# Windowed decode attention with a gated branch: keys turned by VectorE, scores from added shares, two kv heads a unit

## The chip, the cores and the metric

The kernel runs on one core of a Trainium2 chip. The metric is device time in microseconds (us) of one execution. TensorE is PE in the profile (PEld its weight loads), VectorE is DVE, ScalarE is ACT, GpSimd is POOL, and SyncE is SP, which issues nearly all loads here. Everything is float32. PSUM has eight banks of 512 floats a partition.

## The reference

Two tokens (batch 2, one query each) are normalised; one branch attends over the last 4096 keys of a long cache, the other makes a gate.

```
xn = layernorm(x)                                 # x: 2 x 1 x 512
q = xn @ wq                                       # 32 heads of 128
k, v = caches[:, :, -4096:, :]                    # 8 kv heads, 4 query heads each
o = softmax(q @ k.T / sqrt(128)) @ v              # per head
s = o @ wo                                        # 4096 -> 512
z = gelu(xn @ w_in)                               # 1792 wide, halves z1, z2
g = silu((z1 * (w_sp * layernorm(z2) + b_sp)) @ w_out)
out = x + s * g
```

The keys and values used are 2 x 8 x 4096 x 128 floats each, 67.1 MB together; w_in, w_out, wq and wo are 22.3 MB.

## The kernel before, in words

Everything on PE, DVE, ACT and SP is kept in program order by a small wrapper (lines 26 to 38), so the order in the source is the order on each engine. All large loads go through SP's queue into one ring of nine slots of 16 KB a partition (line 74): two halves of w_in, w_out, four quarters of wq, then for each of 16 pairs (batch, kv head) its keys and its values (`load_kv`, line 118), 2 MB each, 16 KB a partition, then wo in seven pieces. A load goes out when the slot's last user is done.

At the start x is normalised and turned; z is made in four pieces of 448 columns, whose four shares are added while PE turns them (28 small products, lines 206 to 210). The products of `queries(0)` to `queries(3)`, one for each quarter of wq, are put between the steps of the gate's branch. Then q is turned on PE into qT.

The loop over pairs (lines 420 to 443) works on pair `cur` while it finishes pair `prev`. For `cur`: 32 transposes of 128x128 on PE (`transposes`, eight groups of four, each into one of three "kt" banks), each group copied to SBUF by DVE or ACT (ON_ACT, line 306); then `scores` (eight products, four column groups of PE beside each other), `row_max` on DVE over 1024 scores, `share_max` on PE. For `prev`: `bias`, `probs` (one exponential of 128x1024 on ACT), `probs_t` (two block transposes of 128x512 on DVE), `share_sum` and `weights`, `pv` (eight products), `evacuate` (four scaled copies on ACT), and one pair later `collect`. So the softmax of one pair and the transposes of the next lie beside each other.

wo is used in three sets of rows (line 296), each with its own turned output (`spread`), so that most of its products can be done before the last pair is through. 24 of the 32 blocks are added in one bank (`part`), the others follow into `so`; then the gate, the addition of x, and two stores.

Of the kernel before, what the change touches and what calls it, by code (L numbers as in the profile page):

```python
# [14 lines left out]
P = 128  # L15
HQ, DH = 32, 128
G = 4
EPS = 1e-5


def free_ap(t, offset, dims):

    return bass.AP(tensor=t.tensor, offset=t.offset + offset, ap=[list(t.ap[0])] + [list(d) for d in dims])
# [18 lines left out]
def kernel(  # L42
# [19 lines left out]
    NT = W // P  # L62
    NR = W // 512 // G
# [3 lines left out]
    FC = F // G  # L67
    FT = FH // P
    NJ = HQ * DH // P
    DC = D // G  # L70
    SCALE = DH ** -0.5

    cst = ctx.enter_context(tc.tile_pool(name="cst", bufs=1))
    ring = ctx.enter_context(tc.tile_pool(name="ring", bufs=9))
# [3 lines left out]
    def slot(name, *shape):  # L78
        return ring.tile([P, *shape], F32, tag="slot", name=name)

    def bank(name, *shape):
        return ps.tile([P, *shape], F32, tag="kt", name=name, bufs=3)


    xs = sb.tile([B, D], F32, tag="o", name="xs")
    act.dma_start(xs, x[:, 0, :])
    win_v = w_in.rearrange("(p k) f -> p k f", p=P)
    win = []
    for a in range(2):
        t = slot(f"win{a}", 2, F)  # L90
        sp.dma_start(t, win_v[:, 2 * a : 2 * a + 2, :])
        win.append(t)
    wout = slot("wout", FT, D)
    sp.dma_start(wout, w_out.rearrange("(p j) d -> p j d", p=P))
    wq_v = wq.rearrange("(p k) f -> p k f", p=P)
    wqt = []
    for a in range(KT):
        t = slot(f"wq{a}", HQ * DH)
        sp.dma_start(t, wq_v[:, a, :])
        wqt.append(t)  # L100
# [4 lines left out]
    x4 = cst.tile([P, DC], F32, tag="x4", name="x4")  # L105
    nc.gpsimd.memset(x4, 0.0)
# [4 lines left out]
    def load_x4():  # L111
        h = DC // 2
        src = bass.AP(tensor=x.tensor, offset=x.offset, ap=[[DC, G], [D, B], [1, h]])
        sp.dma_start(x4[0 : P : P // (G * B), :h], src)
        for b in range(B):
            sp.dma_start(x4[16 * b : P : 32, h:], by_group(x, b, h, DC))

    def load_kv(n):
        b, kv = divmod(n, HKV)
        pair = []  # L120
        for name, src in (("k", k_cache), ("v", v_cache)):
            t = slot(f"{name}{n}", NT, DH)
            sp.dma_start(t, src[b, kv, SK - W :, :].rearrange("(p j) d -> p j d", p=P))
            pair.append(t)
        return pair


    ident = cst.tile([P, P], F32, tag="ident", name="ident")
    make_identity(nc, ident)
    selw = cst.tile([P, 60], F32, tag="selw", name="selw")  # L130
    nc.gpsimd.memset(selw, 0.0)
    xnT = cst.tile([P, KT, 32], F32, tag="xnT", name="xnT")
    nc.gpsimd.memset(xnT, 0.0)
    ones = cst.tile([P, P], F32, tag="ones", name="ones")
    nc.gpsimd.memset(ones, 1.0)
    hT = cst.tile([P, FT, 32], F32, tag="hT", name="hT")
    nc.gpsimd.memset(hT, 0.0)
    qT = cst.tile([P, B * HKV, 32], F32, tag="qT", name="qT")
    nc.gpsimd.memset(qT, 0.0)

    rowm = cst.tile([P, 32], F32, tag="rowm", name="rowm")
    dve.tensor_reduce(rowm, ident.rearrange("p (g c) -> p c g", g=G), axis=AX.X, op=ALU.add)
    grpm = cst.tile([P, G], F32, tag="grpm", name="grpm")
# [20 lines left out]
    xn = sb.tile([B, D], F32, tag="o", name="xn")  # L164
    dve.tensor_scalar(xn, xs, mv[:, 0:1], rs, op0=ALU.subtract, op1=ALU.mult)
    pt = bank("xnT_ps", KT, B)
# [3 lines left out]

    same = cst.tile([P, G, 32], F32, tag="same", name="same")
    dve.tensor_copy(same, free_ap(rowm, 0, [[0, G], [1, 32]]))
    heads = cst.tile([P, 32, REP], F32, tag="heads", name="heads")
    dve.tensor_copy(heads, free_ap(rowm, 0, [[0, 32], [8, REP]]))
    diag = cst.tile([P, 4], F32, tag="diag", name="diag")
    dve.tensor_reduce(diag, free_ap(rowm, 0, [[4, 4], [1, REP]]), axis=AX.X, op=ALU.add)
    dve.tensor_reduce(selw[:, 28:32], free_ap(rowm, 0, [[1, REP], [4, 4]]), axis=AX.X, op=ALU.add)
    perm8 = cst.tile([P, 4, 8, 4, 4], F32, tag="perm8", name="perm8")
    nc.gpsimd.memset(perm8, 0.0)
    for i in range(4):  # L180
        dve.tensor_copy(perm8[:, i, :, :, i], free_ap(ident, 0, [[1, 8], [32, 4]]))
    perm16 = cst.tile([P, 2, 16, 4, 2], F32, tag="perm16", name="perm16")
    nc.gpsimd.memset(perm16, 0.0)
    for i in range(2):
        dve.tensor_copy(perm16[:, i, :, :, i], free_ap(ident, 0, [[1, 16], [32, 4]]))

    assert KT == G
    z = sb.tile([P, F], F32, tag="kts", name="z")  # L190
    for n in range(G):
        pz = bank(f"z{n}", 512)[:, :FC]
        for k in range(KT):
            pe.matmul(
                pz[32 * k : 32 * k + 32, :], xnT[:, k, :], win[k // 2][:, k % 2, n * FC : (n + 1) * FC],
                start=True, stop=True,
            )
        if n % 2:
            dve.tensor_copy(z[:, n * FC : (n + 1) * FC], pz)
        else:  # L200
            act.activation(z[:, n * FC : (n + 1) * FC], pz, AF.Copy)
    wb_ps = ps.tile([P, 512], F32, tag="mo", name="wb_ps")[:, :2]
    pe.matmul(wb_ps, ones[0:1, :], wb1, start=True, stop=True)
    wb = cst.tile([P, 2], F32, tag="wb", name="wb")
    dve.tensor_copy(wb, wb_ps)
    pt = bank("zT_ps", 2, FT, B)
    zv = z.rearrange("b (h p j) -> b h j p", h=2, j=FT)
    for h in range(2):
        for j in range(FT):
            pe.matmul(pt[:, h, j, :], zv[:, h, j, :], rowm[:, :B], start=True, stop=True)  # L210


    assert HKV == NR * G
    pq = ps.tile([P, NR, 512], F32, tag="s", name="q_ps")

    def queries(k):
        for r in range(NR):
            for g in range(G):
                c = (r * G + g) * 512
                pe.matmul(  # L220
                    pq[32 * g : 32 * g + 32, r, :], xnT[:, k, :], wqt[k][:, c : c + 512],
                    start=(k == 0), stop=(k == KT - 1),
                )

    queries(0)
    zT = cst.tile([P, 2, FT, B], F32, tag="zT", name="zT")
    dve.tensor_copy(zT, pt)
    u = cst.tile([P, 2, FT, B], F32, tag="u", name="u")
    dve.tensor_mul(u, zT, zT)
    dve.tensor_scalar(u, u, 0.044715, 1.0, op0=ALU.mult, op1=ALU.add)  # L230
    dve.tensor_mul(u, u, zT)
    dve.tensor_scalar(u, u, -2.0 * math.sqrt(2.0 / math.pi), 80.0, op0=ALU.mult, op1=ALU.min)
    act.activation(u, u, AF.Exp)
    dve.tensor_scalar_add(u, u, 1.0)
    dve.reciprocal(u, u)
    dve.tensor_mul(zT, zT, u)

    z1, z2, w2 = zT[:, 0], zT[:, 1], u[:, 0]
    mean = cst.tile([P, B], F32, tag="mean", name="mean")
    var = cst.tile([P, B], F32, tag="var", name="var")  # L240

    def mean_over_rows(dst, src, name):
        pm = bank(name, FT, B)
        pe.matmul(pm.rearrange("p j b -> p (j b)"), ones, src.rearrange("p j b -> p (j b)"), start=True, stop=True)
        dve.reduce_sum(dst, pm.rearrange("p j b -> p b j"), axis=AX.X)
# [3 lines left out]
    queries(1)  # L249
    dve.tensor_scalar_mul(mean, mean, 1.0 / FH)  # L250
    dve.tensor_sub(z2, z2, free_ap(mean, 0, per_b))
# [4 lines left out]
    dve.tensor_mul(z2, z2, free_ap(mean, 0, per_b))  # L256
    dve.tensor_scalar(z2, z2, wb[:, 0:1], wb[:, 1:2], op0=ALU.mult, op1=ALU.add)
    dve.tensor_mul(hT[:, :, 0 : 16 * B : 16], z1, z2)
    queries(2)
    y = bank("y", DC)  # L260
    for j in range(FT):
        for g in range(G):
            pe.matmul(
                y[32 * g : 32 * g + 32, :], hT[:, j, :], wout[:, j, g * DC : (g + 1) * DC],
                start=(j == 0), stop=(j == FT - 1),
            )
    gate = cst.tile([P, DC], F32, tag="gate", name="gate")
# [6 lines left out]
    queries(3)  # L274
    qs = sb.tile([P, NR, REP, DH], F32, tag="kts", name="qs")
    for r in range(NR):
        dve.tensor_copy(qs[:, r], pq[:, r, :].rearrange("p (i d) -> p i d", i=REP))
    for r in range(NR):
        pt = bank(f"qT_ps{r}", REP, G, 32)
        for i in range(REP):  # L280
            pe.transpose(pt[:, i].rearrange("p g c -> p (g c)"), qs[:, r, i, :], ident)
        for b in range(B):
            dve.tensor_copy(
                qT[:, b * HKV + r * G : b * HKV + r * G + G, ::8], pt[:, :, :, b].rearrange("p i g -> p g i")
            )

    NP = B * HKV
    JH = NT // NR
    acc = ps.tile([P, 4, DH], F32, tag="acc", name="acc")
    dve.memset(acc, 0.0)

    SETS = ((0, 4, 16), (4, 2, 8), (6, 2, 8))
    sets = {}
    for i, (kv, n, nj) in enumerate(SETS):
        o1 = cst.tile([P, B, 32], F32, tag=f"o1_{i}", name=f"o1_{i}")
        oT = cst.tile([P, nj, 32], F32, tag=f"oT_{i}", name=f"oT_{i}")  # L300
        nc.gpsimd.memset(oT, 0.0)
        for a in range(n):
            sets[kv + a] = (a, n, o1)
# [231 lines left out]
```

## Time and profile before

| | |
|---|---|
| Runs | 219.18, 220.66 (median), 221.65 us |
| Span of the profiled execution, first to last instruction | 217.7 us |
| Time of that execution itself | not kept beside its span |
| Instructions | 3816 |
| Busy: PE, DVE, ACT | 176.7, 109.4, 80.5 us |
| Read from HBM | 89.40 MB |
| Loads in flight, issue to landing (values, median) | 36.3 us |

In the profile's rows the engine comes first, then what is written from what is read, its shape, and either a count with the busy time and the mean of one in ns, or a start and a length in us. Brackets at the end of a timeline row are the time that the engine stood idle before it, and who ended that. In a table by stretches the figures are the stretch, its length, busy time (with count) of PE, PEld, DVE, ACT and POOL, the granted TensorE clock as a share of full speed, the share of DMA and GB/s. A float32 product is two records of PE.

### The profile page before, as it was taken

To read this page: it belongs to the slowest core of one execution; us is meant where nothing else is said; L and a number is where in the kernel's file an instruction comes from. 1 tells how busy PE (TensorE), PEld (TensorE's weight loads), DVE (VectorE), ACT (ScalarE), POOL (GpSimd) and SP (SyncE) were. 2 spreads that over 40 slices of the span, in tenths; PEclk is the share of its full clock that TensorE was granted. 3 is DMA by queue.
4 is the path that set the end of the run, shared out by engine and by line. 5 is a ranking of instruction groups with operands and counts; after the bars stand their busy time and mean duration, and the time that the engine had idled before them with its cause. 6 is when DMAs were issued, how large, how long until landed. Compare 5 with 4: busy or idle time off the path is not lost.

```text
span 217.7 us, 3816 instructions
## 1 busy us (share of the span) xinstructions
PE 176.7 (81%) x1554; PEld 105.2 (48%) x1554; DVE 109.4 (50%) x259; ACT 80.5 (37%) x173; POOL 3.6 (2%) x17
## 2 busy tenths in 40 slices
PE   0479996775987979797977979797886899798973
PEld 0127533445572736455462746456372847364232
DVE  3311212853774737575664747575563557476001
ACT  5000202032473544435363544536363236444110
POOL 6000000000000000000000000000000000000000
PEclk9998579996999999999999999999999699999799
DMA  6999999999999999999999999999999999999980
GB/s 238 432 433 434 431 431 428 431 420 431 431 434 428 434 432 425 434 434 431 422 431 428 434 431 431 428 429 428 434 431 431 434 432 420 428 434 425 422 330 12
DMA packets 6693, 89.64 MB, mean 412 GB/s; under 512 B 778, under 2 KB 786, under 8 KB 1172
## 3 DMA queue, kind: packets, MB, share of 16 engines
q1 hardware_dynamic: 6660, 89.40, 96.6%
q8 instruction: 12, 0.20, 0.3%
q14 instruction: 5, 0.04, 0.0%
q10 hardware_dynamic: 16, 0.01, 0.0%
HBM read 89.40 MB, written 0.00 MB: 411 GB/s over the span
## 4 chain that ended last, share of the span: by engine, by line
DMA 71%; PE 24%; DVE 2%; ACT 1%; issue 0%; SPq 0%; ACTq 0%
DMA k<-in_A_k_cache_dram 66%; PE kt L36 8%; DMA win<-in_B_w_in_dram 5%; PE q_ps L36 4%; PE part L36 3%; PE zT_ps L36 3%; PE z L36 2%; PE so L36 1%; PE acc L36 1%; PE s L36 1%; DVE m L36 1%; ACT o L36 1%; ACT p L36 1%; PE oT_ps L36 0%; DVE pT L36 0%
## 5 line engine op out<-in xcount | busy, mean ns | idle before, releaser
L36 PE MATMUL kt<-ident,k 128*128 128x128 f32 x512 | 68.3, 286 | 20.1 <-DMA k<-in_A_k_cache_dram 20.0
L36 PEld LDWEIGHTS kt<-ident,k 128*128 128x128 f32 x512 | 57.8, 145 | 28.3 <-issue 20.2
L36 DVE COPY kts<-kt 128x512 f32<-128x512 f32 x64 | 42.3, 680 | 30.2 <-PE kt L36 21.9
L36 ACT ACTIVATE kts<-kt 128x512 f32<-128x512 f32 x64 | 36.6, 597 | 36.7 <-PE kt L36 36.7
L36 ACT ACTIVATE o<-acc,wd 128x128 f32<-128x128 f32 x64 | 18.2, 368 | 56.1 <-PE acc L36 39.4
L36 PE MATMUL acc<-v,pT 128*16 128x512 f32 x256 | 30.9, 597 | 0.4 <-DVE pT L36 0.4
L36 PE MATMUL s<-kts,qT 128*32 128x512 f32 x256 | 30.8, 598 | 0.0
L36 DVE TENSOR_REDUCE m<-s 128x1 f32<-128x1024 f32 x16 | 19.5, 1222 | 13.4 <-PE s L36 13.4
L36 DVE STREAM_TRANSPOSE pT<-p 128x512 f32<-128x512 f32 x32 | 20.7, 686 | 0.2 <-ACT p L36 0.2
L36 ACT ACTIVATE p<-s,nb 128x1024 f32<-128x1024 f32 x16 | 18.1, 1131 | 3.7 <-DVE nb L36 3.7
L36 PEld LDWEIGHTS acc<-v,pT 128*16 128x16 f32 x256 | 7.9, 109 | 11.2 <-issue 10.8
L36 PEld LDWEIGHTS mo<-mg,same 128*128 128x128 f32 x32 | 4.8, 188 | 16.0 <-DVE mg L36 16.0
L36 PEld LDWEIGHTS s<-kts,qT 128*32 128x32 f32 x256 | 6.6, 108 | 10.0 <-ACT kts L36 7.9
L36 PE MATMUL q_ps<-wq,xnT 128*32 128x512 f32 x64 | 10.3, 773 | 0.0
L36 PE MATMUL z<-win,xnT 128*32 128x448 f32 x32 | 7.1, 895 | 3.6 <-DMA win<-in_B_w_in_dram 3.6
L36 DVE TENSOR_REDUCE o<-col 128x32 f32<-128x128 f32 x6 | 1.7, 292 | 13.7 <-PE col L36 13.7
L36 PEld LDWEIGHTS col<-o,selw 128*32 128x32 f32 x128 | 4.1, 110 | 9.0 <-issue 8.4
L36 PE MATMUL mo<-mg,same 128*128 128x4 f32 x32 | 6.2, 263 | 2.1 <-DVE mg L36 1.6
L36 DVE TENSOR_REDUCE nb<-mo 128x1 f32<-128x4 f32 x16 | 2.6, 162 | 9.9 <-PE mo L36 9.9
L36 PE MATMUL part<-wo,oT 128*32 128x512 f32 x48 | 7.2, 728 | 0.0
L36 PE MATMUL zT_ps<-rowm,z 128*128 128x2 f32 x28 | 6.6, 370 | 0.0
L36 PEld LDWEIGHTS zT_ps<-rowm,z 128*128 128x128 f32 x28 | 6.5, 325 | 0.0
(98 smaller groups left out, 82.8 us busy)
## 6 DMA issues: line engine op xcount, KB each, us to landing
k<-in_A_k_cache_dram SPq DMA_DIRECT2D x16, 2048.0 KB
v<-in_A_v_cache_dram SPq DMA_DIRECT2D x16, 2048.0 KB, 36.3
wq<-in_A_wq_dram SPq DMA_DIRECT2D x4, 2048.0 KB, 28.8
wo<-in_A_wo_dram SPq DMA_DIRECT2D x3, 2048.0 KB
win<-in_B_w_in_dram SPq DMA_DIRECT2D x2, 1792.0 KB, 7.3
wout<-in_B_w_out_dram SPq DMA_DIRECT2D x1, 1792.0 KB
wo<-in_A_wo_dram SPq DMA_DIRECT2D x1, 1024.0 KB
wo<-in_A_wo_dram SPq DMA_DIRECT2D x1, 512.0 KB, 18.2
```

Source lines behind the costliest of these rows:

```text
L36: return self.tc.keep_in_program_order(call(*args, **kwargs))
```

## The change

The loop is rewritten. Names of the changed kernel are used.

- Loads. The ring has four slots of 32 KB a partition instead of nine of 16 KB. w_in is one load of 28 KB rows, wq two loads, wo one load of 32 KB rows, one of 16 KB and four smaller ones. A unit is two kv heads of one batch; its keys (and its values) are one load of 4 MB, where partition 2i + a holds 64 keys of head a (`load_unit`). The order is k0, k1, v0, k2, v1 and so on.
- Keys. PE's transposes and the copies out of PSUM are gone. DVE turns 16 keys a partition at a time in blocks of 32x32 (`turn`, 128x2048, four a unit, two buffers). Such a block has 32 of the 128 head dimensions, so `shares` makes for each quarter `dq` of the dimensions a product of its own into 32 partitions of one bank; ACT copies the bank to SBUF, and `add_shares` adds the four quarters with a full 128x128 product of 512 columns.
- Scores of a key stand for the query heads of both kv heads; those of the wrong one are masked by a bias of -1e30 (`negm`). `row_max` works on two halves with a step of two; `probs` is two exponentials of 128x1024 with a step of two; `probs_t` two block transposes of 128x1024; `values` 16 products; `scale_out` as `evacuate` before; `collect` four products into one column group.
- Order. One unit is carried nearly to its end before the next: only `turn` 0 and 1 of the next unit stand ahead of `probs_t`, and `shares` of the next unit stand behind `values`.
- Start and end. z comes from 16 products into one bank, in shares that DVE turns; w_out and wo are used with whole rows of 512. All queries stand behind the gate, are turned by DVE and spread by products with masks. wo is one set of rows, with one turned output `oT`; 28 blocks go into `part`, four into `so`.

The core of the diff:

```
+    ring = ctx.enter_context(tc.tile_pool(name="ring", bufs=4))
...
+        src = bass.AP(tensor=first.tensor, offset=first.offset, ap=[[SLOT, P // 2], [SK * DH, 2], [1, SLOT]])
+        sp.dma_start(t, src)
...
+    def turn(u, m):
+        u.kt[m] = sb.tile([P, JC, DH], F32, tag="kt", name=f"kt{u.n}_{m}")
+        dve.transpose(
+            u.kt[m].rearrange("p j d -> p (j d)"), u.k[:, JC * m : JC * m + JC, :].rearrange("p j d -> p (j d)")
+        )
+    def shares(u, m):
+        u.sh = bank(f"sh{u.n}_{m}", "sh")
+        for dq in range(4):
+            pe.matmul(
+                u.sh[32 * dq : 32 * dq + 32, :], q_of(u, dq), u.kt[m][:, :, 32 * dq : 32 * dq + 32],
+                start=True, stop=True,
+            )
+        u.shs[m] = sb.tile([P, 512], F32, tag="shs", name=f"shs{u.n}_{m}")
+        act.activation(u.shs[m], u.sh, AF.Copy)
+    def add_shares(u, m):
...
+        pe.matmul(u.s[:, m, :], add_dq, u.shs[m], start=True, stop=True)
...
+    def share_max(u):
+        t = sb.tile([P, 2], F32, tag="t", name=f"t{u.n}")
+        dve.tensor_scalar_mul(t, u.m4[:, :, 0], am[:, 0:1])
+        dve.scalar_tensor_tensor(t, u.m4[:, :, 1], am[:, 1:2], t, op0=ALU.mult, op1=ALU.add)
+        mg = sb.tile([P, 2, G], F32, tag="mg", name=f"mg{u.n}")
+        dve.tensor_mul(mg, ap(t, 0, [[1, 2], [0, G]]), ap(grpm, 0, [[0, 2], [1, G]]))
+        u.mo = bank(f"mo{u.n}", "mo")
+        pe.matmul(u.mo[:, : 2 * G], same, mg.rearrange("p a g -> p (a g)"), start=True, stop=True)
+        mx = sb.tile([P, 1], F32, tag="mx", name=f"mx{u.n}")
+        dve.reduce_max(mx, u.mo[:, : 2 * G], axis=AX.X)
+        u.nb = sb.tile([P, 2], F32, tag="nb", name=f"nb{u.n}")
+        dve.scalar_tensor_tensor(u.nb, ap(mx, 0, [[0, 2]]), -SCALE, negm, op0=ALU.mult, op1=ALU.add)
...
+    prev = None
+    for u in units:
+        if prev is None:
+            turn(u, 0)
+            turn(u, 1)
+        shares(u, 0)
+        shares(u, 1)
+        if prev is not None:
+            scale_out(prev)
+        add_shares(u, 0)
+        turn(u, 2)
+        shares(u, 2)
+        add_shares(u, 1)
+        turn(u, 3)
+        shares(u, 3)
+        add_shares(u, 2)
+        if prev is not None:
+            collect(prev)
+        row_max(u, 0)
+        add_shares(u, 3)
+        row_max(u, 1)
+        share_max(u)
+        probs(u)
+        nxt = units[u.n + 1] if u.n + 1 < NU else None
+        if nxt is not None:
+            turn(nxt, 0)
+            turn(nxt, 1)
+        probs_t(u, 0)
+        probs_t(u, 1)
+        weights(u)
+        values(u)
+        prev = u
+    scale_out(prev)
+    collect(prev)
```

More of the change, by code (lines that the diff above doesn't have):

```diff
@@ L118, in load_kv, with load_unit @@
[L118 to L128, printed above, removed]
+    def load_unit(cache, u, name):
+        b, w = divmod(u, NU // B)
+        t = slot(f"{name}{u}")
+        first = cache[b, 2 * w, SK - W :, :]
+        src = bass.AP(tensor=first.tensor, offset=first.offset, ap=[[SLOT, P // 2], [SK * DH, 2], [1, SLOT]])
+        sp.dma_start(t, src)
+        return t.rearrange("p (j d) -> p j d", d=DH)
@@ L178 @@
[L178 to L190, printed above, removed]
@@ L191 @@
-    for n in range(G):
-        pz = bank(f"z{n}", 512)[:, :FC]
-        for k in range(KT):
+    same = const("same", G, 32)
+    dve.tensor_copy(same, ap(rowm, 0, [[0, G], [1, 32]]))
+    same = same.rearrange("p g c -> p (g c)")
+    heads = const("heads", 16, 8)
+    dve.tensor_copy(heads, ap(rowm, 0, [[0, 16], [4, 8]]))
+    heads = heads.rearrange("p x r -> p (x r)")
+    diag = const("diag", 4)
+    dve.tensor_reduce(diag, rowm.rearrange("p (j r) -> p j r", j=4), axis=AX.X, op=ALU.add)
+    dve.tensor_reduce(sel[:, 3:35:4], rowm.rearrange("p (j r) -> p r j", j=4), axis=AX.X, op=ALU.add)
@@ new lines @@
+    for a in range(2):
+        dve.tensor_copy(add_dq[:, :, 16 * a : 16 * a + 16 : 4], rowm[:, 16 * a : 16 * a + 16].rearrange("p (g h) -> p g h", g=G))
+    add_dq = add_dq.rearrange("p g r -> p (g r)")
+    am = const("am", 2)
+    dve.tensor_reduce(am, ap(rowm, 0, [[16, 2], [4, REP]]), axis=AX.X, op=ALU.add)
+    negm = const("negm", 2)
+    dve.tensor_scalar(negm, am, -1.0, BIG, op0=ALU.add, op1=ALU.mult)
+    FQ = FH // G
+    pz = bank("z", "sh")[:, : 2 * FQ]
+    for k in range(KT):
+        for g in range(G):
@@ L203 @@
+                start=(k == 0), stop=(k == KT - 1),
+            )
+    wb_ps = bank("wb_ps", "mo")[:, :2]
     pe.matmul(wb_ps, ones[0:1, :], wb1, start=True, stop=True)
-    wb = cst.tile([P, 2], F32, tag="wb", name="wb")
+    wb = const("wb", 2)
     dve.tensor_copy(wb, wb_ps)
[L206 to L210, printed above, removed]
@@ L213 @@
[L213 to L227, printed above, removed]
@@ L272 @@
     dve.tensor_mul(gate, gate, y)
[L274 to L281, printed above, removed]
+    pq = ps.tile([P, 2, 512], F32, tag="s", name="q_ps")
+    for k in range(KT):
+        for r in range(2):
+            for g in range(G):
+                c = (r * G + g) * 512
+                pe.matmul(
+                    pq[32 * g : 32 * g + 32, r, :], xnT[:, k, :], wqt[k // 2][:, k % 2, c : c + 512],
+                    start=(k == 0), stop=(k == KT - 1),
+                )
@@ L324, in scores @@
-    def scores(p, r):
-        if r == 0:
-            p.s = ps.tile([P, NR, 512], F32, tag="s", name=f"s{p.n}")
+            dve.tensor_scalar_mul(
+                ap(qm, b * 128 + gs // 2 * 32 + gs % 2 * 4, [[64, 2], [8, 4], [1, REP]]),
+                ap(qT, b, [[512, 2], [32, 4], [128, REP]]), grpm[:, gs : gs + 1],
+            )
+    rp = bank("rp", "mo")[:, : 2 * B * 64]
+    pe.matmul(rp, same, qm, start=True, stop=True)
+    qbd = const("qbd", B * 2 * G * 4, G, REP)
+    for g in range(G):
+        dve.tensor_scalar_mul(qbd[:, :, g, :], rp.rearrange("p (x h) -> p x h", h=REP), grpm[:, g : g + 1])
@@ new lines, in probs, with probs_t @@
+    def probs(u):
+        u.p = sb.tile([P, J, 32], F32, tag="p", name=f"p{u.n}", bufs=1)
+        u.l = sb.tile([P, 2], F32, tag="l", name=f"l{u.n}")
+        for a in range(2):
+            act.activation(
+                ap(u.p, a, [[2, J * 16]]), ap(u.s, a, [[2, J * 16]]), AF.Exp,
+                bias=u.nb[:, a : a + 1], scale=SCALE, accum_out=u.l[:, a : a + 1],
+            )
+    def probs_t(u, half):
+        if half == 0:
+            u.pT = sb.tile([P, J, 32], F32, tag="pT", name=f"pT{u.n}", bufs=1)
+        h = slice(J // 2 * half, J // 2 * (half + 1))
+        dve.transpose(u.pT[:, h].rearrange("p j r -> p (j r)"), u.p[:, h].rearrange("p j k -> p (j k)"))
@@ new lines, in weights, with values @@
+    def weights(u):
+        pe.matmul(u.mo[:, 2 * G : 2 * G + 2], heads, u.l, start=True, stop=True)
+        l = sb.tile([P, 1], F32, tag="ls", name=f"ls{u.n}")
+        dve.reduce_sum(l, u.mo[:, 2 * G : 2 * G + 2], axis=AX.X)
+        dve.reciprocal(l, l)
+        u.wd = sb.tile([P, 4], F32, tag="wd", name=f"wd{u.n}")
+        dve.tensor_scalar_mul(u.wd, diag, l)
+    def values(u):
+        u.acc = bank(f"acc{u.n}", "acc")
+        NQ = J // 4
+        for q in range(NQ):
+            c = q % G
+            pe.matmul(
+                u.acc[32 * c : 32 * c + 32, :], ap(u.pT, 4 * q * 32, [[4, 32]]),
+                u.v[:, 4 * q : 4 * q + 4, :].rearrange("p j d -> p (j d)"), start=(q < G), stop=(q >= NQ - G),
+            )
@@ new lines, in scale_out, with collect @@
+    def scale_out(u):
+        u.o = sb.tile([P, 4, DH], F32, tag="o", name=f"o{u.n}")
+        for jj in range(4):
+            act.activation(
+                u.o[:, jj, :], u.acc[:, jj * DH : (jj + 1) * DH], AF.Copy, scale=u.wd[:, jj : jj + 1]
+            )
+    col = {}
+    def collect(u):
+        if u.w == 0:
+            col[u.b] = bank(f"col{u.b}", "col")[:, : 4 * 32].rearrange("p (j d) -> p j d", j=4)
+        for e in range(4):
+            pe.matmul(
+                col[u.b][32 * u.w : 32 * u.w + 32], sel[:, 3 - e : 35 - e], u.o[:, :, 32 * e : 32 * e + 32],
+                start=(e == 0), stop=(e == 3),
+            )
+        if u.w == NU // B - 1:
+            dve.reduce_sum(oT[:, :, 16 * u.b], col[u.b].rearrange("p j d -> p d j"), axis=AX.X)
@@ new lines @@
+    units = []
+    for n in range(NU):
+        u = Unit()
+        u.n, u.kt, u.shs = n, {}, {}
+        u.b, u.w = divmod(n, NU // B)
+        units.append(u)
+    for n in range(NU + 1):
+        if n < NU:
+            units[n].k = load_unit(k_cache, n, "k")
+        if n > 0:
+            units[n - 1].v = load_unit(v_cache, n - 1, "v")
+    wo_v = wo.rearrange("(p j) d -> p j d", j=32)
+    blocks = []
+    pieces = ((16,), (8,), (4, 2, 1, 1))
+    j = 0
+    for i, piece in enumerate(pieces):
+        t = slot(f"wo{i}").rearrange("p (j d) -> p j d", d=D)
+        at = 0
+        for n in piece:
+            sp.dma_start(t[:, at : at + n, :], wo_v[:, j : j + n, :])
+            blocks += [(t, at + a) for a in range(n)]
+            at, j = at + n, j + n
+            if j == 16:
+                for b in range(B):
+                    sp.dma_start(x4[16 * b : P : 32, :], by_group(x, b, 0, DC))
@@ new lines @@
+    scale_out(prev)
+    collect(prev)
+    EARLY = 28
+    part = bank("part", "sh")
+    for n in range(EARLY):
+        t, a = blocks[n]
+        g = n % G
+        pe.matmul(part[32 * g : 32 * g + 32, :], oT[:, n, :], t[:, a, :], start=(n < G), stop=(n >= EARLY - G))
+    parts = sb.tile([P, D], F32, tag="shs", name="parts")
+    act.activation(parts, part, AF.Copy)
+    so = bank("so", "mo")[:, :DC]
+    spread_quarters(so, parts, stop=False)
+    for n in range(EARLY, 32):
+        t, a = blocks[n]
@@ L460, in wo_early @@
-    def wo_early(n):
-        nonlocal done
-        t, oT, j = blocks[n]
-        for a in range(t.shape[1]):
-            g = done % G
-            pe.matmul(
-                part[32 * g : 32 * g + 32, :], oT[:, j + a, :], t[:, a, :], start=(done < G), stop=(done >= EARLY - G)
-            )
-            done += 1
-    last = pairs[-1]
-    bias(last)
-    probs(last)
-    spread(0)
-    spread(1)
-    probs_t(last, 0)
-    probs_t(last, 1)
-    collect(old)
-    share_sum(last)
-    weights(last)
```

338 lines of the change are left out of this document (94 added, 244 removed).

## The prediction

> **What bounds the kernel now.** I read the page first: the busy shares, the rate of the slices and the chain that ended last.
>
> ```profile
> span 217.7 us, 3816 instructions
> ...
> PE 176.7 (81%) x1554; PEld 105.2 (48%) x1554; DVE 109.4 (50%) x259; ACT 80.5 (37%) x173; POOL 3.6 (2%) x17
> ...
> GB/s 238 432 433 434 431 431 428 431 420 431 431 434 428 434 432 425 434 434 431 422 431 428 434 431 431 428 429 428 434 431 431 434 432 420 428 434 425 422 330 12
> ...
> HBM read 89.40 MB, written 0.00 MB: 411 GB/s over the span
> ...
> DMA 71%; PE 24%; DVE 2%; ACT 1%; issue 0%; SPq 0%; ACTq 0%
> ```
>
> PE looks busiest, but the chain is 71% DMA: from the second slice to the 38th the loads run at 420 to 434 GB/s without a hole. 89.4 MB at that rate are the kernel. The timeline of three pairs in the middle shows how much room the engines have beside it:
>
> ```profile
> 100.35 4.14 PE L36 MATMUL kt<-ident,k 128*128 128x128 f32 x32 [1.16 <-DMA k<-in_A_k_cache_dram]
> ...
> 110.03 4.14 PE L36 MATMUL kt<-ident,k 128*128 128x128 f32 x32 [1.32 <-DMA k<-in_A_k_cache_dram]
> ...
> 119.76 4.14 PE L36 MATMUL kt<-ident,k 128*128 128x128 f32 x32 [1.21 <-DMA k<-in_A_k_cache_dram]
> ```
>
> A pair takes 9.7 us (100.35 to 110.03 to 119.76), which is its 4.19 MB at 432 GB/s, and in each PE waits 1.2 to 1.3 us for keys. So the pair's own loop needs about 8.5 us: spare, but only an eighth. The span is 217.7; no time of that execution is kept beside it, and the median of the runs (219.18 to 221.65) is 220.66, so I take 3.0 us to lie around the span and add them at the end.
>
> **The loads.** Bytes are the same. Large loads go from 46 to 26, rows from 14 to 16 KB to 28 to 32 KB. The slices already hold 431 to 434 with the short rows, queued one behind another, so I take nothing from the longer rows; the most they could give is 434 for the mean of the steady slices, about 1%, some 2 us. A unit (two pairs) is 8.39 MB: 19.4 us at 432 GB/s. That is the number that the unit's loop has to beat. Landing times: 1.3 MB in the first slice of 5.4 us, then 432 GB/s; k0 ends at 18.1 MB, 44.3 us; v0 at 26.5 MB, 63.7 us; v of unit 6 at 180.4 us.
>
> **The unit's loop.** The new order is serial: with two kt buffers, turn 2 waits for shares 0, which stands on PE behind all of values of the unit before, which waits for that unit's probs_t, which stands on DVE behind two turns of the next unit. So I add up one round. The durations, from the groups by form and from the timeline:
>
> ```profile
> L36 DVE STREAM_TRANSPOSE pT<-p 128x512 f32<-128x512 f32 x32 | 20.7, 686 | 0.2 <-ACT p L36 0.2
> L36 DVE TENSOR_REDUCE m<-s 128x1 f32<-128x1024 f32 x16 | 19.5, 1222 | 13.4 <-PE s L36 13.4
> L36 ACT ACTIVATE kts<-kt 128x512 f32<-128x512 f32 x64 | 36.6, 597 | 36.7 <-PE kt L36 36.7
> L36 ACT ACTIVATE p<-s,nb 128x1024 f32<-128x1024 f32 x16 | 18.1, 1131 | 3.7 <-DVE nb L36 3.7
> L36 PE MATMUL mo<-mg,same 128*128 128x4 f32 x32 | 6.2, 263 | 2.1 <-DVE mg L36 1.6
> L36 PEld LDWEIGHTS mo<-mg,same 128*128 128x128 f32 x32 | 4.8, 188 | 16.0 <-DVE mg L36 16.0
> L36 DVE TENSOR_SCALAR mg<-grpm,m 128x4 f32<-128x4 f32 x16 | 3.7, 230 | 0.6
> L36 DVE TENSOR_REDUCE nb<-mo 128x1 f32<-128x4 f32 x16 | 2.6, 162 | 9.9 <-PE mo L36 9.9
> ```
> ```profile
> 103.13 1.29 DVE L36 STREAM_TRANSPOSE pT<-p 128x512 f32<-128x512 f32 x2
> ...
> 104.54 1.93 PE L36 MATMUL s<-kts,qT 128*32 128x512 f32 x16
> ...
> 106.28 0.40 PE L36 MATMUL col<-o,selw 128*32 128x128 f32 x8
> ...
> 106.50 1.90 PE L36 MATMUL acc<-v,pT 128*16 128x512 f32 x16
> 106.53 1.23 DVE L36 TENSOR_REDUCE m<-s 128x1 f32<-128x1024 f32 x1 [1.19 <-PE s L36]
> ...
> 108.33 0.39 PE L36 MATMUL mo<-mg,same 128*128 128x4 f32 x2
> 108.46 1.14 ACT L36 ACTIVATE o<-acc,wd 128x128 f32<-128x128 f32 x4 [3.34 <-PE acc L36]
> ```
>
> The last fence's second row is eight products (two records each) in four column groups: 0.96 us for a set of four. From s (ending at 106.47) to m (106.53) a hand-over costs 0.06.
>
> - turn, 128x2048 on DVE: not in the trace. Upper end four short ones back to back, 4 x 0.645 = 2.58. One alone is 0.686, and m shows that DVE takes 0.536 for 512 elements more (1.222 - 0.686): 0.686 + 3 x 0.536 = 2.29, less the 0.04 by which a following one overlaps (0.686 to 0.645): 2.25. I take that, as one instruction starts once; the upper end is 1.3 us more a unit.
> - probs_t, 1024 elements: 1.2 each. row_max, 1024 from PSUM with a step of two: 1.22 as m; the step is not in the trace, from 0 to double; I take 0, since m is one element a cycle already.
> - shares: 0.96, the copy 0.6, on one bank, so each shares waits for the copy before it.
> - add_shares: a full 128x128 stationary and 512 columns, not in the trace. Lower end 0.86 (two records of a set), upper end the set's 0.96 and two exposed loads of 0.15 (188 ns is the mean): 1.26. I take 0.96, the nearest row in columns streamed.
> - collect: four products, now all in one column group, so one after another: between 0.4 (four groups) and four times the 0.4; I take 0.9.
> - share_max: 0.23 + 0.2 + 0.2 on DVE, 0.39 on PE, 0.16 + 0.2 on DVE, hand-overs: 1.5.
>
> One round, 0 being the end of the second probs_t. PE: the first half of values starts at -1.1 behind the first probs_t, each half is 1.9, done at 2.7; shares 0 at 3.7. DVE stands still until then but for 0.6 of weights. Turn 2 to 6.0, turn 3 to 8.2. PE meanwhile: shares 1 (behind copy 0) 5.35, add 0 6.3, shares 2 7.3, add 1 8.25, shares 3 9.2, add 2 10.2, collect 11.1, add 3 12.05. DVE: row_max 0 at 9.5, then a wait for add 3; row_max 1 at 13.3; share_max 14.8; two turns of the next unit 19.3 (the exponentials, 2 x 1.13 on ACT, lie under them); probs_t 21.7. **A round is 21.7 us, against 19.4 us of loads**: 15.4 of it DVE at work, 3.1 waiting for values and shares 0, 2.6 for add 3, 0.5 for the maximum's product. scale_out (1.14) and the copies lie on ACT beside PE; without that cover scale_out would delay copy 2.
>
> PE has a hole of 8.5 us in each round (12.05 to 20.6) with two small products in it. What such a hole does, the trace shows by a smaller one:
>
> ```profile
> 49.24 0.39 PE L36 MATMUL mo<-mg,same 128*128 128x4 f32 x2 [1.61 <-DVE mg L36]
> 51.58 5.12 PE L36 MATMUL kt<-ident,k 128*128 128x128 f32 x32 [1.95 <-DMA k<-in_A_k_cache_dram]
> ```
> ```profile
> 50.00:52.00 2.00, 0.42 (x2) 0.45 (x3) 0.02 (x1) 1.21 (x2) 0.00 (x0) 0.72 0.99 426
> 52.00:54.00 2.00, 2.00 (x12) 2.00 (x11) 1.13 (x2) 0.00 (x0) 0.00 (x0) 0.50 1.03 442
> 54.00:56.00 2.00, 2.00 (x18) 1.84 (x16) 1.39 (x3) 1.23 (x3) 0.00 (x0) 0.93 1.04 442
> ```
>
> After some 4 us with only mo in them, the next 32 transposes take 5.12 instead of 4.14: the granted clock (third figure from the right) is 0.50 for about 3.4 us (0.28 x 2 / 0.5, then 2, then 0.07 x 2 / 0.5) and then full again. With a hole of 8.5 us I expect this in every unit, and it falls on values and shares 0, which are on the path: 3.4 us at half speed lose 1.7 us. A round is then 23.4 us. The Trainium skill (TensorE: Matmul & The Clock Gate, Part 1) says that an idle window of about 3.4 us halves the clock and that a busy one restores it, the windows running freely. By that rule PE could stay slow for up to two windows after the hole, an estimate of 3.4 us lost a unit and some 13 us more in all; the trace's holes agree with one window, and the sum keeps that.
>
> **Loads under this loop.** Four slots: the keys of unit n+2 go out when turn 3 of unit n is done (8.2 in the round) and are turned first 30 us later; two loads ahead of them or with them take 19.4. That is cover enough; the slots cost nothing while a round is longer than 19.4. SP waits in order for each slot, and nothing of the compute stands behind it.
>
> **Start and end.** From the timeline:
>
> ```profile
> 12.27 5.40 PE L36 MATMUL z<-win,xnT 128*32 128x448 f32 x28 [2.42 <-DMA win<-in_B_w_in_dram]
> ...
> 24.44 3.64 PE L36 MATMUL q_ps<-wq,xnT 128*32 128x512 f32 x16
> 24.54 0.19 DVE L36 COPY zT<-zT_ps 128x28 f32<-128x28 f32 x1 [6.13 <-PE zT_ps L36]
> ...
> 31.61 1.92 PE L36 MATMUL q_ps<-wq,xnT 128*32 128x512 f32 x16
> ...
> 35.21 0.18 DVE L36 TENSOR_TENSOR hT<-zT 128x14 f32<-128x14 f32 x1
> ```
> ```profile
> 209.07 1.92 PE L36 MATMUL part<-wo,oT 128*32 128x512 f32 x16
> ...
> 211.13 0.60 ACT L36 ACTIVATE parts<-part 128x512 f32<-128x512 f32 x1 [4.14 <-PE part L36]
> ...
> 212.02 1.93 PE L36 MATMUL so<-wo,oT 128*32 128x128 f32 x64
> ...
> 214.66 0.56 SPq L36 DMA_DIRECT2D out_dram<-res  x1
> ```
>
> The 28 transposing products of z go (6.5 us), but the queries now stand behind the whole gate on PE. z 12.3 + 32 records at 0.193 = 18.5; copy and turn 1.4; the chain to hT was 10.85 with two waits behind queries, from 7 to 10.85 now, I take 7.7; y and its quarters 4.6; queries, 64 records, half at 0.23 and half at 0.12: 11; turning and spreading q about 5. Together 48; not before k0 (44.3), at most 51. Unit 0 then takes four turns and the rest of a round, 21.3: its second probs_t ends at 69.3. Six rounds follow, and a last one without the next unit's turns (2 us less). Then values 2.7, scale_out 1.14, collect 0.9, its sum 0.3, 56 records of part 6.7, copy 0.6, so 1.2, two DVE operations 0.6, hand-overs 0.5, and 3.0 from the out load's issue to the span's end (214.66 to 217.7): 17.6. With r the round, **time = 3 + 69.3 + 6r + (r - 2) + 17.6 = 87.9 + 7r**; for r = 23.4, and 1.7 more for the last values at half clock, 253.4. The new part with one set of wo (no spread, one reduce a batch) saves spread's 1.1 us; it is left out of the 17.6.
>
> **Rivals.**
> - The clock stays full, or returns before values matter: r = 21.7, 240 us. For it: small products lie in the hole. Against it: mo lay in the 4 us hole too.
> - The other side: the loads still bind, and it is a little faster. Then t(unit 6) is 180.4 by the loads, and the time is 180.4 + (r - 2) + 17.6 + 3 = 199 + r, or 216.5 at r = 17.5; it decides at r below 18.9, where 87.9 + 7r crosses 220.66. That needs waits of under 3.5 us beside DVE's 15.4; values' second half and shares 0 alone leave 3.1, add 3 another 2.6. For it: before, DVE and PE overlap so well that a pair has 1.2 us to spare. [...]
> - Rows of two heads 16 MB apart read slower. It binds below 8.39 MB / 23.4 us = 358 GB/s; at 300 a unit takes 28 us and the time is about 285. Against it: wq's rows, 64 KB apart, ran at 431 to 434 in slices 3 to 7.
>
> **How the numbers follow.** Forecast 0.62 (r from 22.6 to 24.9: 248 to 264), full clock 0.22 (232 to 243), slow rows 0.04, loads bind 0.07, and 0.05 for a round that happens to fall near 19 us. Under 1% either way could not be told from no change. Slower 0.88, same 0.05, faster 0.07. The range reaches down into the full-clock case, to r = 21.2, and up to both upper ends in part: 236 to 264.
>
> **What would show it.** Right: slices near 360 GB/s instead of 431; the chain on DVE and PE instead of DMA; DVE waiting some 3 us or more for shares 0 and 2 to 3 for add 3 in each of eight rounds of 22 to 25 us; turns at 2.25; PE's clock near 0.5 for 3 us behind each hole. Wrong: turns waiting for loads of k, a round under 19.5, or a set of four values products at 0.96 us right behind the hole.

## The result, and the profile after

The changed kernel takes 263.9 us, median of four runs (262.86 to 264.93), against 220.08 us for the kernel before (219.18 to 221.65): 1.197 times, with a 95% interval of 1.190 to 1.205. The prediction was 253, from 236 to 264, so the result lies at the upper end of that range. The profiled execution took 264.93 us, of which 263.1 are its span.

The page of the kernel after, the lines that answer to those shown first of before:

```profile
span 263.1 us, 2303 instructions
...
PE 160.1 (61%) x898; PEld 49.3 (19%) x898; DVE 136.1 (52%) x191; ACT 54.8 (21%) x109; POOL 2.5 (1%) x13
...
PEclk9996577577569858965995799569858975997698
...
GB/s 280 427 450 438 438 412 453 408 438 433 428 446 408 463 408 354 453 399 323 239 418 458 162 398 399 473 5 398 403 466 90 418 458 323 209 376 53 0 2 1
...
PE 57%; DVE 31%; ACT 5%; DMA 4%; issue 2%; ACTq 0%; DVEq 0%
```

The chain has left the loads (71% before, 4% now) and lies on PE and DVE in turn, with neither busy for more than 61% of the span. The loads run at full rate until the 15th slice and then show gaps down to 5 GB/s: they wait for slots (SP's queue stood 120.9 us for the values that free one and 43.0 us for turns). PE's clock swings in every unit. That is the picture of two engines that work one after the other.

One round in the timeline of the kernel after (start, length, engine, work; in brackets the idle time before and its releaser):

```profile
119.83 2.33 DVE L37 STREAM_TRANSPOSE pT<-p 128x1024 f32<-128x1024 f32 x2
...
121.08 5.35 PE L37 MATMUL acc<-v,pT 128*32 128x512 f32 x32 [2.46 <-DVE pT L37]
...
126.25 1.03 PE L37 MATMUL sh<-kt,qbd 128*32 128x512 f32 x8
...
127.36 4.50 DVE L37 STREAM_TRANSPOSE kt<-k 128x2048 f32<-128x2048 f32 x2 [4.70 <-PE sh L37]
...
133.17 1.12 PE L37 MATMUL s<-shs,add_dq 128*128 128x512 f32 x2
...
134.34 1.22 DVE L37 TENSOR_REDUCE m<-s 128x2 f32<-128x1024 f32 x1 [2.47 <-PE s L37]
...
135.71 1.10 PE L37 MATMUL s<-shs,add_dq 128*128 128x512 f32 x2 [0.42 <-DVE m L37]
136.84 1.22 DVE L37 TENSOR_REDUCE m<-s 128x2 f32<-128x1024 f32 x1 [1.28 <-PE s L37]
...
139.75 4.50 DVE L37 STREAM_TRANSPOSE kt<-k 128x2048 f32<-128x2048 f32 x2
...
144.17 2.33 DVE L37 STREAM_TRANSPOSE pT<-p 128x1024 f32<-128x1024 f32 x2
145.43 5.12 PE L37 MATMUL acc<-v,pT 128*32 128x512 f32 x32 [2.47 <-DVE pT L37]
```

Read it by the waits. DVE ends probs_t at 122.16 and, but for half a microsecond of weights, stands until 127.36, while PE makes values (5.35 us; 3.67 with a full clock, 29.4 / 8 in the first experiment) and shares 0. Then row_max 0 starts 0.05 us after the sum at 133.17 has ended, which is add 2; and the last sum, add 3, starts only when row_max 0 is done (134.34 + 1.22 = 135.56). DVE waits again. From its end at 136.81 to 145.43 PE has two small products.

The start of `nb` (the bias with the maximum, one a unit) in each of the eight units gives the rounds, and DVE's waits between 66 and 216 us (in total, times, longest) say what fills six of them:

```profile
L37 DVE SCALAR_TENSOR_TENSOR nb<-mx,negm x8: 160/160/161, 65.3 to 238.5; 128x2 f32<-128x2 f32 x8
```
```profile
DVE kt L37 <- PE sh L37: 30.7, 6, 5.8
DVE m L37 <- PE s L37: 20.0, 11, 2.5
DVE mx L37 <- PE mo L37: 3.5, 6, 0.7
DVE oT L37 <- PE col L37: 3.5, 1, 3.5
```

From 65.27 to 214.48, where the seventh `nb` starts, are six rounds: 24.87 us each. Waits take 5.1 (values and shares 0), 3.9 (the maxima; with the one for oT, the turned output of a batch, which stands in place of one of them), 0.6 (the maximum's product), 9.6 in all; DVE works 15.0, and 0.2 are hand-overs.

### The profile page after: what moved, and what is told of

Its sections match the earlier page's. It is cut to its first block, busy times and chain, and to the rows that moved or that the text cites. A ratio compares the mean times of both kernels' runs of the same rounds, so it can differ in the third digit from the quotient of the medians.

```text
span 263.1 us, 2303 instructions
## 1 busy us (share of the span) xinstructions
PE 160.1 (61%) x898; PEld 49.3 (19%) x898; DVE 136.1 (52%) x191; ACT 54.8 (21%) x109; POOL 2.5 (1%) x13
## 4 chain that ended last, share of the span: by engine, by line
PE 57%; DVE 31%; ACT 5%; DMA 4%; issue 2%; ACTq 0%; DVEq 0%
PE acc L37 17%; PE s L37 13%; PE sh L37 13%; DVE kt L37 13%; DVE m L37 7%; DMA win<-in_B_w_in_dram 4%; DVE pT L37 4%; PE q_ps L37 3%; PE part L37 2%; PE z L37 2%; ACT shs L37 2%; PE mo L37 2%; DVE t L37 1%; PE y L37 1%; ACT p L37 1%
## 5 line engine op out<-in xcount | busy, mean ns | idle before, releaser
L37 DVE STREAM_TRANSPOSE kt<-k 128x2048 f32<-128x2048 f32 x32 | 72.0, 2289 | 35.6 <-PE sh L37 35.6
L37 PE MATMUL acc<-v,pT 128*32 128x512 f32 x256 | 45.9, 880 | 18.0 <-DVE pT L37 18.0
L37 ACT ACTIVATE shs<-sh 128x512 f32<-128x512 f32 x32 | 19.1, 597 | 115.3 <-PE sh L37 115.3
L37 PE MATMUL sh<-kt,qbd 128*32 128x512 f32 x256 | 36.1, 639 | 10.3 <-ACT shs L37 6.2
L37 PE MATMUL s<-shs,add_dq 128*128 128x512 f32 x64 | 36.7, 656 | 5.6 <-DVE m L37 5.6
L37 DVE TENSOR_REDUCE m<-s 128x2 f32<-128x1024 f32 x16 | 19.6, 1224 | 29.3 <-PE s L37 29.3
L37 ACT ACTIVATE p<-s,nb 128x1024 f32<-128x1024 f32 x16 | 18.5, 1169 | 48.2 <-DVE nb L37 48.2
L37 DVE STREAM_TRANSPOSE pT<-p 128x1024 f32<-128x1024 f32 x16 | 18.7, 1205 | 2.5 <-ACT p L37 2.5
L37 PEld LDWEIGHTS acc<-v,pT 128*32 128x32 f32 x256 | 10.4, 158 | 46.8 <-issue 28.2
L37 PEld LDWEIGHTS s<-shs,add_dq 128*128 128x128 f32 x64 | 9.7, 191 | 29.5 <-issue 29.5
L37 PE MATMUL mo<-mg,same 128*128 128x8 f32 x16 | 4.0, 321 | 16.3 <-DVE mg L37 16.3
L37 ACT ACTIVATE o<-acc,wd 128x128 f32<-128x128 f32 x32 | 9.1, 373 | 7.5 <-PE acc L37 7.5
## 6 DMA issues: line engine op xcount, KB each, us to landing
wq<-in_A_wq_dram SPq DMA_DIRECT2D x2, 4096.0 KB, 29.4
```

The lines of the kernel that those rows point to most:

```text
L37: return self.tc.keep_in_program_order(call(*args, **kwargs))
```

## The experiments

Theory: the time comes from the serial order (DVE stands while PE makes values, shares 0 and the last sums) and from the half clock behind PE's hole (called cold below), which falls on values. Rivals: the loads (interleaved rows, four large slots) set the time; or the new instructions themselves are too much work, whatever their order. All ratios are to runs of the kernel before that were made beside the experiment.

**The hole filled.** 28 products a unit whose sums are thrown away go into PE's hole, two sets of four behind add 3 and five behind the maximum's product:

```
         add_shares(u, 3)
+        warm(u, 2, "a")
         row_max(u, 1)
         share_max(u)
+        warm(u, 5, "b")
         probs(u)
```

> The changed kernel, with 28 products a unit added whose sums are thrown away (two sets of four behind add 3, five sets behind the maximum's product), so that PE has no long hole; nothing else moves. Theory (the halved clock behind the hole lies on the path): values' 16 products fall from 5.7 us on the mean to about 3.9, the round from 24.9 to about 23.0, the time from 264 to 249 (245 to 254). Rival (the clock is off the path, the round is set by DVE or by the loads): 262 to 266, although the clock is full.

Measured: 248.1 us, ratio 1.126 (1.119 to 1.133), mean granted clock 0.94 instead of 0.79. Turns and values of this kernel, in the groups (busy, mean ns | idle before):

```profile
L37 DVE STREAM_TRANSPOSE kt<-k 128x2048 f32<-128x2048 f32 x32 | 72.0, 2289 | 21.9 <-PE sh L37 21.7
...
L37 PE MATMUL acc<-v,pT 128*32 128x512 f32 x256 | 29.4, 598 | 9.1 <-issue 9.1
```

The same two groups in the kernel after, and two more that are needed below:

```profile
L37 DVE STREAM_TRANSPOSE kt<-k 128x2048 f32<-128x2048 f32 x32 | 72.0, 2289 | 35.6 <-PE sh L37 35.6
L37 PE MATMUL acc<-v,pT 128*32 128x512 f32 x256 | 45.9, 880 | 18.0 <-DVE pT L37 18.0
...
L37 PE MATMUL sh<-kt,qbd 128*32 128x512 f32 x256 | 36.1, 639 | 10.3 <-ACT shs L37 6.2
...
L37 DVE TENSOR_REDUCE m<-s 128x2 f32<-128x1024 f32 x16 | 19.6, 1224 | 29.3 <-PE s L37 29.3
```

So more work on PE made the kernel 15.8 us shorter: values win 16.5 us over eight units, and DVE's wait for them falls by 13.9. The half clock is on the path, with some 2 us a unit. The other 28 us stay.

**Shares 0 and 1 ahead of values.** Each stands behind its turn, so that turn 2 need not wait for values:

```
+            turn(nxt, 0)
+            shares(nxt, 0)
+            turn(nxt, 1)
+            shares(nxt, 1)
         probs_t(u, 0)
```

(the two `shares` at the head of the loop are left for unit 0 only).

> The changed kernel with one order changed on PE: shares 0 and 1 of the next unit stand ahead of values of this one, right behind their turns, so that turn 2 no longer waits for values. Theory (the serial order is the cost): DVE's 4.5 us of idle time before turn 2 goes nearly to zero, but add 3 then comes after values and becomes the later wait, so 3 us a round are won and not 4.5: 238 to 244. Rival (loads or DVE's own work set the round): under 5 us won, 259 to 264.

Measured: 254.07 us, ratio 1.154 (1.148 to 1.160); a miss. The groups:

```profile
L37 DVE STREAM_TRANSPOSE kt<-k 128x2048 f32<-128x2048 f32 x32 | 72.0, 2287 | 2.1 <-DMA k<-in_A_k_cache_dram 1.7
L37 PE MATMUL sh<-kt,qbd 128*32 128x512 f32 x256 | 48.0, 832 | 31.2 <-DVE kt L37 25.2
L37 DVE TENSOR_REDUCE m<-s 128x2 f32<-128x1024 f32 x16 | 19.6, 1224 | 45.1 <-PE s L37 45.1
L37 PE MATMUL acc<-v,pT 128*32 128x512 f32 x256 | 41.8, 811 | 0.7 <-DVE pT L37 0.7
```

The wait that it aimed at is gone (35.6 to 2.1), and the next one is longer (29.3 to 45.1): the sums stand behind values. PE restarts earlier with shares, and now these run partly at half clock (832 ns a record instead of 639), and values still do (811). So an order alone gives 9.8 us, because the cold stretch moves along with the first work behind the hole.

**Both.** The order of the last experiment, with two and three sets of four thrown-away products in the hole:

> Shares 0 and 1 of the next unit ahead of values, as in the earlier run of that order, and PE's holes filled (two sets of four products behind add 3, three behind the maximum's product; their sums are thrown away). That order alone gave 254.1 where 238 to 244 was expected, with shares at 1.94 us a set behind the hole. Theory (the missing part was the halved clock, on shares and values that now both stand ahead of add 0): a round of about 20 us, 226 to 234. Rival (the two costs overlap, so filling adds only what it gave alone beside the order's 10 us, or less): 238 or more.

Measured: 230.76 us, ratio 1.050 (1.043 to 1.057), clock 0.955.

```profile
L37 DVE STREAM_TRANSPOSE kt<-k 128x2048 f32<-128x2048 f32 x32 | 72.0, 2287 | 1.9 <-DMA k<-in_A_k_cache_dram 1.6
...
L37 DVE TENSOR_REDUCE m<-s 128x2 f32<-128x1024 f32 x16 | 19.6, 1224 | 32.8 <-PE s L37 32.8
```

33.1 us are won, more than 9.8 and 15.8 together: with either cost undone alone, part of the other's gain stays hidden. What is left above all is the wait for the sums, 4.1 us a unit.

**row_max 0 as soon as its scores are there,** ahead of shares 3 and add 2, and collect behind the maximum's product:

```
         turn(u, 3)
+        row_max(u, 0)
         shares(u, 3)
         add_shares(u, 2)
-        if prev is not None:
-            collect(prev)
-        row_max(u, 0)
         add_shares(u, 3)
         row_max(u, 1)
         share_max(u)
+        if prev is not None:
+            collect(prev)
```

> The changed kernel with row_max 0 moved ahead of add 2 and add 3 in the program, and collect behind the maximum's product. Theory (add 3 is held by row_max 0 and by collect, neither of which it needs): row_max 0 starts right behind turn 3, DVE's idle time before the maxima falls from 3.7 to about 2.6 us a round, and 1.0 to 1.5 us a round are won: 252 to 257. Rival (that wait is off the path): 262 to 266.

Measured: 254.35 us, ratio 1.157 (1.150 to 1.165).

```profile
L37 DVE STREAM_TRANSPOSE kt<-k 128x2048 f32<-128x2048 f32 x32 | 72.0, 2289 | 38.1 <-PE sh L37 37.4
...
L37 DVE TENSOR_REDUCE m<-s 128x2 f32<-128x1024 f32 x16 | 19.6, 1224 | 21.4 <-PE s L37 21.4
```

The wait before the maxima falls from 29.3 to 21.4, and six rounds of `nb` (63.63 to 205.19) take 23.6 us each instead of 24.9. In this kernel row_max 0 starts right behind add 1, and the next sum starts only when row_max 0 is done. So the wait for add 2 in the changed kernel comes from the place of row_max 0 in the source, not from its scores: the scores are one tile (`u.s`), and its reader waits for the last writer ahead of it in the source. Collect was moved in the same run; that add 3 was held by row_max 0 and not by collect is read from the changed kernel's row (0.42 us, ended by m), not tested alone.

**Most of the work left out.** All loads stay:

> All loads of the changed kernel in their order and slots, but three of four turns, three of four shares and three of four sets of values are left out, so a round of compute is about 15 us. Theory (the loads of 32 KB rows of two heads run as fast as the short rows and were never the bound): 428 to 434 GB/s in the slices and 213 to 221 us. Rival (interleaved long rows or four slots slow the loads): below 400 GB/s and 230 us or more. If long rows are better by themselves: above 436 GB/s.

Measured: 220.71 us, ratio 1.002 (0.998 to 1.006). The page:

```profile
GB/s 255 426 439 465 399 465 403 435 429 429 441 429 441 429 441 411 453 411 447 417 444 417 417 447 423 447 425 441 423 447 420 441 405 459 405 453 393 416 313 1
...
DMA 69%; PE 20%; DVE 4%; ACT 4%; issue 2%; ACTq 0%
```

With three quarters of the turns, shares and values out of the way the changed loads give the time of the kernel before: 26 large loads instead of 46, most of them with rows of 28 to 32 KB, two heads 16 MB apart. The slices swing more (393 to 465 GB/s from the second to the 38th), but taken together the changes to the loads neither cost nor win anything here, and the rival of slow rows falls. Nor does a fixed cost of each load show: with twenty loads fewer the ratio is 1.002.

**Values one round later,** with the orders of the two experiments on shares and on row_max, and scale_out and collect ahead of probs_t, so that values too lie under DVE's turns:

```
         share_max(u)
+        if prev is not None:
+            values(prev)
         probs(u)
...
+            shares(nxt, 1)
+        if prev is not None:
+            scale_out(prev)
+            collect(prev)
         probs_t(u, 0)
         probs_t(u, 1)
         weights(u)
-        values(u)
```

> The changed kernel with the orders of the two experiments on shares and on row_max, and values of a unit behind the maximum's product of the next one, in PE's hole; scale_out and collect follow it. Same instructions, other order. Theory (serial order is the cost, the parts themselves are not): DVE waits under 4 us a round, a round is 18.4 to 19.5, about the loads' 19.4, and the time is 218 to 232, about that of the kernel before. Rival (the added work of turns and added shares is itself too much): above 240.

Measured: 253.16 us, ratio 1.153 (1.149 to 1.156); a miss. Two waits show why, one that was not there before and one that stayed:

```profile
L37 DVE TENSOR_REDUCE m<-s 128x2 f32<-128x1024 f32 x16 | 19.6, 1225 | 29.1 <-PE s L37 29.0
...
L37 DVE TENSOR_REDUCE ls<-mo 128x1 f32<-128x2 f32 x8 | 1.2, 155 | 17.6 <-PE mo L37 17.6
```

Weights are needed by nobody until scale_out, a round later. But their product now stood on PE behind collect, which waited for scale_out on ACT; and DVE, in order, stood at `ls` 2.5 us a unit (seven times), with turn 2 behind it. The wait before the maxima is as long as in the changed kernel (21.4 us with row_max early alone), and the sums took 810 ns a record instead of 656, at a mean clock of 0.82. By its time alone this run would speak for the rival; the next one decides.

**The same instructions in an order meant to avoid these waits.** Shares ahead, values after the next unit's maximum, weights after turn 3, scale_out at the loop's head, row_max 0 early, collect last:

```
+        if old is not None:
+            scale_out(old)
         add_shares(u, 0)
...
         turn(u, 3)
-        shares(u, 3)
-        add_shares(u, 2)
         if prev is not None:
-            collect(prev)
+            weights(prev)
         row_max(u, 0)
+        shares(u, 3)
+        add_shares(u, 2)
         add_shares(u, 3)
+        if old is not None:
+            collect(old)
         row_max(u, 1)
         share_max(u)
+        if prev is not None:
+            values(prev)
...
-        weights(u)
-        values(u)
-        prev = u
+        old, prev = prev, u
```

> The changed kernel with its instructions in another order, mended after the order with late values: shares 0 and 1 of the next unit behind their turns, values and weights one round later (values in PE's hole behind the maximum's product, weights behind turn 3, where nothing waits for them), row_max 0 ahead of add 2, collect in the hole behind add 3. Theory (the order is the cost, in two ways: DVE waits for PE, and PE's holes halve its clock): DVE's own 15.5 us and 2.5 to 3 us of waits make a round of 18 to 19, under the loads' 19.4; slices near 430 GB/s and 217 to 228 us. Rival (turns and added shares are too much work in themselves): 235 or more.

Measured: 219.09 us, ratio 0.995 (0.991 to 0.999). DVE still has 191 instructions and PE 898. Its seven rounds as stretches of the profiled execution (220.80 us, the longest of ten), from `nb` to `nb` (the stretch, its length, busy time of PE, PEld, DVE, ACT and POOL, clock, DMA share, GB/s):

```profile
63.99:81.88 17.89, 11.73 (x48) 3.18 (x52) 14.90 (x16) 4.79 (x8) 0.00 (x0) 0.81 0.98 422
81.88:99.78 17.90, 13.21 (x88) 4.68 (x84) 14.91 (x17) 5.97 (x12) 0.00 (x0) 1.00 1.00 428
99.78:117.67 17.89, 13.20 (x88) 4.68 (x84) 14.90 (x16) 5.98 (x12) 0.00 (x0) 1.00 1.02 437
117.67:136.73 19.06, 14.76 (x88) 5.18 (x84) 14.90 (x16) 5.99 (x12) 0.00 (x0) 0.91 1.00 430
136.73:156.09 19.36, 13.41 (x88) 4.88 (x84) 15.10 (x18) 5.99 (x12) 0.00 (x0) 0.97 1.00 431
156.09:175.97 19.88, 16.14 (x88) 4.93 (x84) 15.02 (x16) 5.87 (x12) 0.00 (x0) 0.86 1.00 430
175.97:195.29 19.32, 14.76 (x88) 5.20 (x84) 14.90 (x16) 5.98 (x12) 0.00 (x0) 0.91 1.00 430
```

The mean is 18.8 us instead of 24.9, with the same 14.9 to 15.1 us of DVE in it, and the loads run at 422 to 437 GB/s all the time. So the rival that the new instructions are too much work falls: in this order they fit beside the loads. DVE's waits have fallen to 1.0 us before turns, 16.3 before the maxima and 4.2 at `ls`, in all eight units. The second and third round, at a full clock, take 17.9 us; the first takes as long at 0.81, but without values. The last four take 19.1 to 19.9, at 0.86 to 0.97, and no engine is seen to wait for keys or values there: their waits are still those of PE and DVE on each other.

**Two variants of it,** with one set of dummy products behind collect, and with a second buffer for the turned probabilities as well:

> The same with four products a unit added behind collect, whose sums are thrown away, so that PE's last hole is filled as well. If the clock of the kernel without them is below 0.95 and the round above 19.4 there, this is 3 to 10 us faster than it; if the loads bind already, the two are within 1%.

> The best order so far, with its filled hole, and two buffers for pT instead of one, so that the second-to-last values no longer hold probs_t (5 us in all of DVE's waits in the order without filling). The loads bind there, so the rounds gain nothing; the last unit's probs_t comes up to 0.8 us earlier. Expected 217 to 219, that is, not to be told from the run without it; a gain of over 1% on the kernel before would need the loads to end earlier.

Measured: 218.91 us, ratio 0.994 (0.991 to 0.997), and 218.73 us, ratio 0.995 (0.993 to 0.998). The set moved the mean clock only from 0.899 to 0.904, so it is no test of a warm loop. In the lightened kernel, in the reordered one and in the last variant alike the rate falls off at about 210 us, and the spans are 216.8, 219.0 and 216.7: what is still to be won in the loop lies within some 2 us of what these loads allow. That the loads alone set the last variants' time is not shown: the chain that ended last is still PE 34%, DVE 34% and DMA 19% in the last variant. None of the kernels beats the one before by 1%.

## Why the prediction was right, and where it was off

It named the side and the mechanism: slower, because a serial round of DVE and PE is longer than the loads, with a half clock on values. The loads of the loop fell to 368 GB/s (66 to 216 us), near the 360 that it named as a sign. That the time lies inside the range at all is partly luck. The range ended at 264 for prices in part at their upper ends; two of the four runs lie above that, the median 0.1 us below, and what filled the range was not those prices but an order that the prediction had wrong. By its own steps, predicted and measured in the profiled execution (264.93):

| Step | Predicted | Measured | Difference |
|---|---|---|---|
| First turn | 48 | 46.3 | |
| Unit 0's second probs_t ends | 69.3 | 72.1 | +2.8 |
| Six rounds | 6 x 23.4 | 6 x 24.87 | +8.8 |
| Last round | 21.4 | 22.25 | +0.9 |
| Tail, with cold values | 19.3 | 19.5 | +0.2 |
| Around the span | 3.0 | 1.8 | -1.2 |
| Sum | 253.4 | 264.9 | +11.5 |

- **Prices held within their bounds.** Turn 2.25 in a pair (4.50 for two), probs_t 1.2 (1.205), row_max with its step 1.22 (1.224), sums 0.96 (1.10 to 1.13, between the stated 0.86 and 1.26), collect 0.9 (1.06); the last two are 15 to 18% above what was taken.
- **The step that was off** is the round's row of maxima: "row_max 0 at 9.5, then a wait for add 3". It had row_max 0 run as soon as its own two sums were there, and only row_max 1 wait. The trace has row_max 0 wait for add 2 and add 3 wait for row_max 0: 3.9 us instead of 2.6. The early row_max 0 shows it from the other side: there row_max 0 runs early, as the prediction reckoned (collect stands elsewhere, and add 2 too waits for row_max 0); the waits are 2.7 us a unit and a round is 23.6, against the predicted 2.6 and 23.4.
- **The half clock** was priced at 1.7 us a unit on values and shares 0; values alone lose 2.06 (45.9 less 29.4, by eight), between that and its estimate of 3.4 for two windows. DVE's wait before turn 2 was 5.1, not 4.8. DVE's own work was 15.0, not 15.4.
- **Unit 0.** Its first shares and sums run behind a hole as well, at half clock, which the prediction left out; it began turning 1.7 us early and ended 2.8 us late.
- **Rivals.** A full clock was priced at r = 21.7 and 240 us; with the hole filled a round is 22.7 (six from 65.26 to 201.47) and the time 248.1, as the wait for the maxima stays (29.4 us). The loads bind below r = 18.9, the prediction said; the reordered kernel has 18.8 and stands within 1% of before. Slow rows fall with the lightened kernel; wq's rows, held against them, ran at 428 to 434 in slices 3 to 7, not 431 to 434.
- **Loads.** Taken at nothing gained: 1.002.

## What to carry to other kernels

When a change replaces an overlapped loop by a serial one, add up one round engine by engine, each wait with what stands ahead of it on its engine in program order, and hold the sum against the loads of a round; the price list alone (15 us of DVE against 19.4 us of loads) would have said that it fits. Two costs on the same path, here an order and a cold clock, are not told apart by removing one: undo each alone and both together. And when work is moved to hide it, look at what becomes the first work behind the hole, and at the small product that now waits behind it.

## What was not expected of the hardware

A hole of 2 us was enough to halve the clock. Stretches of the kernel after, where the last sum ends at 136.81 and the next product starts at 138.84, and where values restart at 121.08:

```profile
137.00:138.00 1.00, 0.00 (x0) 0.00 (x0) 1.00 (x1) 0.00 (x0) 0.00 (x0) 1.00 0.61 262
138.00:139.00 1.00, 0.16 (x1) 0.16 (x1) 0.68 (x4) 0.00 (x0) 0.00 (x0) 0.61 1.22 524
139.00:140.00 1.00, 0.43 (x2) 0.34 (x2) 0.49 (x3) 0.07 (x1) 0.00 (x0) 0.50 1.21 524
```
```profile
123.00:124.00 1.00, 1.00 (x12) 0.19 (x4) 0.00 (x0) 0.00 (x0) 0.00 (x0) 0.50 0.11 33
124.00:125.00 1.00, 1.00 (x12) 0.19 (x8) 0.00 (x0) 0.00 (x0) 0.00 (x0) 0.72 0.00 0
125.00:126.00 1.00, 1.00 (x16) 0.38 (x12) 0.00 (x0) 0.00 (x0) 0.00 (x0) 1.00 0.00 0
```

The clock falls at about 138.2, 1.4 us into the hole (0.61 is 0.22 of that stretch at full and 0.78 at half), and returns at about 124.6, 3.5 us after PE restarted. The Trainium skill (TensorE: Matmul & The Clock Gate, Part 1) says that the clock halves after an idle window of about 3.4 us and that the windows run freely. The return agrees with that length, and 124.6 and 138.2 lie four times 3.4 us apart. The fall does not agree: the 3.4 us before it held 1.6 us of products (the end of collect, and add 3), so the window was not idle, and here the measurement decides.

The length of the hole alone does not tell what follows. In the reordered kernel a hole of 2.05 us before 126.84 halved the clock (0.83 from 127 to 128, then 0.50), and one of 2.05 us before 145.90 did not (1.00 from 143 to 148). Nor is the price the same in every unit: values take 5.1 to 6.5 us in the kernel after, against 3.67 at a full clock.

The exponentials on ACT take 1169 ns in the kernel after and 1245 with PE busy beside them (the filled hole). The cause is not tested here.
